# Named places for the temporary tiles of a list-scheduled stretch, with new tables of its plan

## The chip, the cores and the metric

The kernel runs on one core of a Trainium2 chip. The metric is the time of one execution on the device in microseconds. Before the change the median of three runs is 1575.53 us (1574.72 to 1575.8).

## What is computed

Attention in chunks of 64 positions feeds two feed-forward layers of 4608 tokens, width 512 and inner width 2048, the first with h cos h, the second with a sigmoid form of gelu. All of it is in float32.

```python
scores = scale * np.matmul(q_c, k_c.transpose(0, 1, 2, 4, 3))     # 8 batches, 8 heads, 9 chunks of 64
scores = scores - np.max(scores, axis=-1, keepdims=True)
attn = np.exp(scores)
attn = attn / (np.sum(attn, axis=-1, keepdims=True) + 1e-09)
out = np.matmul(attn, v_c)
...
h = x @ w_in
g = h * np.cos(h)
x = g @ w_out
h = x @ moe2_w_in
g = h * (1.0 / (1.0 + np.exp(-1.702 * h)))
out = g @ moe2_w_out
```

## The kernel before

The 4608 tokens are worked on in nine slices of 512. A product in float32 accuracy is made of three: each operand is split in a high and a low part, and high by high, high by low and low by high are summed in PSUM. The kernel begins with a **planned part** (`first_stretch`, up to about 330 us of the trace) and goes on with pairs of slices whose products are formed with fewer multiplications; for these, sums of weight slices ("left factors") and of activations ("right factors") are made ahead.

In the planned part a small list scheduler, the class `Plan`, puts operations on five engines in an order, by an estimated duration of each, a longest path and tables of numbers (`RANK`, `LEAN`, `LEFT` and others). The instructions are then issued in that order, and every engine executes its own in order. The operations are:

- Attention by pairs of token blocks, numbered 0 to 9: scores on TensorE (L395), maximum, subtraction and sum on VectorE (L419, L423, L434), exponentials on ScalarE (L431, or L443 as 16 small ones that give their sums too, for the pairs in `EXP_SUM`), normalisation (L453), transposes on TensorE (L477), their copy by ScalarE (L484, tile `pt`), products with the values (L504, tile `x`). Small products that only keep TensorE working, the fillers (L386), stand ahead of some steps.
- Conversion of 32 weight slices, i0 to i15 of the first layer's w_in and o0 to o15 of its w_out, from float64 bits: absolute value by ScalarE into a temporary tile `wt` (L289), four steps of VectorE (L292, L297, L303, L309), the high part by ScalarE (L320), the low part by VectorE (L326) or, for those in `BY_DMA`, by ScalarE and an adding DMA issued by GpSimd (L331, L334).
- First products `h` (L594, one step of 12 matmuls for each weight slice and token slice) and the cosine (L618 to L633), whose result `r` is stored to memory (`gd<-r`, SyncE, L651).
- Reload ("get", `gt<-gd`, L1565), split in `gh` (ScalarE, L1569) and `gl` (VectorE, L1573), and second products `y` (L686); a flush of the finished `y` goes by VectorE or ScalarE (L713, L715; table `FLUSH`) and a store.
- Left factors: sums of two weight slices (`w32`, L817; `su`, `sw`, L765), split in parts `s_part` (L784, L787) and stored (`wc<-s_part`, L768), with stores of the plain parts beside them (`wc<-i`); later they are loaded back as `w_xh`, `w_xl` (L859). Stores `wo` put the second weights away. Right factors `x_b`, `x_t` and their intermediate `chain` (L887 to L893).
- The plan ends with `joint`: the first products of the first pair of slices (`pb`, `pu`, `pc`, L1191). Their copy by ScalarE (`part<-pb`, L1208) and the sum on VectorE (`part<-pu,part`, L1212) come from code behind the plan, where the order of TensorE is written out and the other engines are ordered by the scheduler of the language.

Temporary tiles of 256 KB (`wt`, `pt`, `r`, `gt`, `yo`, `w32`, `su`, `sw`, `s_part`, `chain`) come from one pool of eight buffers, in the planned part and behind it. The plan counts eight places and does not name them: which buffer a tile gets is settled by the pool, and its first writer waits until the last reader of the tile before it, an engine or a DMA, is done.

## Time and profile before

| what | value |
|---|---|
| median of three runs | 1575.53 us |
| the profiled execution | 1577.51 us |
| its span in the trace | 1575.7 us |
| TensorE busy | 1537.0 us (98%) |
| VectorE busy | 1101.3 us (70%) |
| ScalarE busy | 943.0 us (60%) |
| bytes moved | 414.46 MB, mean 263 GB/s |

The span is the time between the first and the last recorded instruction, the profiled execution's own time is 1.8 us longer. A busy time of 98% says that TensorE sets the length as a whole; it doesn't say in which stretch it waits. For a change to one stretch, the waits of TensorE in that stretch are the view to open, and then what the releaser of the longest wait did itself wait for.

### The profile page before, as it was taken

The page shows a single profiled execution, that of the slowest core. Times are in us where ns is not written, and L with a number is a line of the kernel's source. Part 1 is how long each engine was busy: PE and PEld are TensorE (multiplying, and loading weights), DVE is VectorE, ACT ScalarE, POOL GpSimd, SP SyncE. Part 2 cuts the span into 40 slices and gives each one's busy share as a digit, 9 for nine tenths or more (in the row PEclk, how much of TensorE's full clock was granted, in tenths as well). Part 3 has the DMA queues.
Part 4 walks back from the last instruction along what each step waited for, and adds up shares of the span by engine and source line. Part 5 has one row for each costly group of instructions (what it writes and reads, how often), then busy time and mean ns, then how long its engine had stood idle before and what let it go on. Part 6 is the DMA issues. An engine that isn't in the chain of part 4 may idle for free.

```text
span 1575.7 us, 23982 instructions
## 1 busy us (share of the span) xinstructions
PE 1537.0 (98%) x8919; PEld 1263.8 (80%) x8919; DVE 1101.3 (70%) x1830; ACT 943.0 (60%) x1701; POOL 20.8 (1%) x29
## 2 busy tenths in 40 slices
PE   7799999979999999999999999999999999999998
PEld 6688888768888888788887877888888888888887
DVE  7788876777876787767764886478348834773466
ACT  7788764447775777657773654565356445644453
POOL 0000000000000000000000110000000000000000
PEclk9999999989999999999999999999999999999999
DMA  9753589999888689868989999576667665666663
GB/s 381 261 201 128 160 314 340 335 308 325 307 289 320 228 306 301 334 211 275 321 314 340 315 289 295 214 274 230 218 222 268 210 220 216 239 221 215 231 212 136
DMA packets 141189, 414.46 MB, mean 263 GB/s; under 512 B 13712, under 2 KB 28048, under 8 KB 127760
## 3 DMA queue, kind: packets, MB, share of 16 engines
q1 hardware_dynamic: 137760, 406.90, 73.7%
q0 software_dynamic: 3312, 6.03, 2.1%
q8 instruction: 70, 1.15, 0.3%
q14 instruction: 47, 0.39, 0.1%
HBM read 318.77 MB, written 88.08 MB: 258 GB/s over the span
## 4 chain that ended last, share of the span: by engine, by line
PE 84%; DMA 8%; DVE 5%; ACT 2%; issue 1%; SPq 1%; ACTq 0%; DVEq 0%
PE y L686 20%; PE q L1098 19%; PE pu L1033 11%; PE pu L1191 8%; PE h L594 8%; PE pc L1033 5%; PE pc L1191 4%; PE pb L1033 3%; PE pb L1191 2%; DMA gt<-gd 1%; DMA wc<-s_part 1%; PE x L504 1%; DMA wq<-s_part 1%; PE s L395 1%; DMA raw_o<-w_out 1%
## 5 line engine op out<-in xcount | busy, mean ns | idle before, releaser
L686 PE MATMUL y<-gh,wo 128*128 128x512 f32 x768 | 202.9, 393 | 1.0 <-DMA wo<-wo 1.0
L1098 PE MATMUL q<-gf,w_q 128*128 128x512 f32 x768 | 179.3, 389 | 0.0
L1098 PEld LDWEIGHTS q<-gf,w_q 128*128 128x128 f32 x768 | 144.2, 188 | 29.9
L686 PEld LDWEIGHTS y<-gh,wo 128*128 128x128 f32 x768 | 142.4, 188 | 31.6 <-issue 1.2
L1033 PE MATMUL pu<-x_t,w_s 128*128 128x512 f32 x576 | 141.8, 390 | 0.7 <-DVE part L1008 0.7
L686 PE MATMUL y<-gh,o 128*128 128x512 f32 x512 | 132.6, 393 | 1.2 <-DVE yo L713 1.1
L1015 ACT ACTIVATE g<-part 128x512 f32<-128x512 f32 x96 | 60.5, 631 | 111.1 <-DVE part L1008 111.1
L1033 PEld LDWEIGHTS pu<-x_t,w_s 128*128 128x128 f32 x576 | 108.1, 188 | 23.5 <-DVE part L1008 1.1
L1098 PE MATMUL q<-gh,w_q 128*128 128x512 f32 x384 | 124.2, 389 | 0.0
L686 PEld LDWEIGHTS y<-gh,o 128*128 128x128 f32 x512 | 94.9, 188 | 21.7 <-DVE yo L713 1.6
L686 PE MATMUL y<-gl,wo 128*128 128x512 f32 x384 | 105.9, 390 | 0.0
L1191 PE MATMUL pu<-x_t,w_xh 128*128 128x512 f32 x288 | 90.3, 395 | 7.8 <-DVE part L1212 7.8
L1164 ACT ACTIVATE r<-r 128x512 f32<-128x512 f32 x96 | 60.5, 630 | 41.8 <-DVE r L1161 41.6
L686 PEld LDWEIGHTS y<-gl,wo 128*128 128x128 f32 x384 | 72.1, 188 | 15.7 <-DVE gl L264 0.8
L1098 PEld LDWEIGHTS q<-gh,w_q 128*128 128x128 f32 x384 | 72.1, 188 | 15.0
L594 PE MATMUL h<-xh,i 128*128 128x512 f32 x256 | 83.7, 401 | 0.0
L264 DVE TENSOR_TENSOR gf<-g,gf 128x512 fp32r<-128x512 f32 x68 | 46.9, 692 | 40.4 <-ACT gf L263 40.3
L1098 PE MATMUL q<-gl,w_q 128*128 128x512 f32 x192 | 74.8, 389 | 0.0
L1008 DVE TENSOR_TENSOR part<-pu,part 128x512 f32<-128x512 f32 x64 | 44.2, 691 | 39.6 <-PE pu L1033 21.3
L686 PE MATMUL y<-gl,o 128*128 128x512 f32 x256 | 70.7, 390 | 1.2 <-DVE gl L646 1.2
L1191 PEld LDWEIGHTS pu<-x_t,w_xh 128*128 128x128 f32 x288 | 54.0, 190 | 20.8 <-DVE part L1212 9.6
L1008 DVE TENSOR_TENSOR part<-pc,part 128x512 f32<-128x512 f32 x32 | 22.1, 691 | 63.5 <-PE pc L1033 62.1
(174 smaller groups left out, 3259.0 us busy)
## 6 DMA issues: line engine op xcount, KB each, us to landing
w_s<-wc SPq DMA_DIRECT2D x64, 1024.0 KB, 6.1
w_q<-wq SPq DMA_DIRECT2D x56, 1024.0 KB, 5.0
wo<-wo SPq DMA_DIRECT2D x96, 512.0 KB, 5.2
w_xh<-wc SPq DMA_DIRECT2D x24, 1024.0 KB, 7.1
w_xl<-wc SPq DMA_DIRECT2D x24, 1024.0 KB, 9.3
qk<-qk SPq DMA_DIRECT2D x36, 512.0 KB, 7.1
raw_i<-w_in SPq DMA_DIRECT2D x32, 512.0 KB, 7.6
raw_o<-w_out SPq DMA_DIRECT2D x32, 512.0 KB, 7.7
```

The costliest lines, as they stand in the source:

```text
L264: nc.vector.tensor_tensor(out=lo, in0=src, in1=hi.bitcast(F32), op=ALU.subtract)
L395: nc.tensor.matmul(out=s[e][o0:o0 + CH, w, h, :], lhsT=t[p0:p0 + CH, 0, h, o0:o0 + CH], rhs=t[p0:p0 + CH, 1, h, o0:o0 + CH],)
L504: nc.tensor.matmul(out=xs[i][o0:o0 + CH, b, w, c * CH:(c + 1) * CH], lhsT=t[p0:p0 + CH, c, b, e, :], rhs=pt[p0:p0 + CH, e * (HP // 2) + b, ...
L594: nc.tensor.matmul(out=h, lhsT=a[:, w0], rhs=b[k % 2][:, k // 2] if (layer, j) == (0, 2) else b[:, k, :], start=(k == 0 and i == 0), stop= ...
L686: nc.tensor.matmul(out=ys[d0], lhsT=a, rhs=b, start=(f == 0 and i == 0), stop=(f == NF - 1 and i == 2),)
L1008: nc.vector.tensor_tensor(out=t, in0=more, in1=t, op=ALU.add)
L1015: nc.scalar.activation(out=dest, in_=h, func=AF.Gelu_apprx_sigmoid)
L1033: nc.tensor.matmul(out=o, lhsT=x, rhs=y, start=(m < 3 and k == 0 and n == 0), stop=(m in (1, 5, 6) and k == 1 and n == 2), skip_group_chec ...
L1098: nc.tensor.matmul(out=o, lhsT=x, rhs=y, start=(m < 3 and i == 0 and k == 0), stop=(m in (1, 5, 6) and i == NP - 1 and k == 2), skip_group ...
L1164: nc.scalar.activation(out=r, in_=r, func=AF.Sin, scale=math.pi)
L1191: nc.tensor.matmul(out=out, lhsT=x, rhs=y, start=(start and k == 0 and n == 0), stop=(stop and k == 1 and n == 2), skip_group_check=True,)
```

## The change

Each temporary tile of the planned part now has a named place, `t0` to `t7`. `Plan` chooses it when it puts the operation in the order: of the places that are free, the one that came free first, and a place whose tile is last read by a DMA counts as free when the plan believes the transfer to have landed (before: a fixed 2.0 us after an issue by SyncE, 3.5 by GpSimd). The places form a pool of their own that is closed behind the planned part; a new pool `tmp` of eight buffers is opened behind it on the same memory. The intermediate `chain` of the first pair's t1 moves from a temporary buffer to the pool `ap`. The tables of the plan are new: among them `LEFT` (how far along the second products each left factor begins), `LF_AT` (when the factors are loaded back), `WO`, `FLUSH` (two instead of five flushes by VectorE), `EXP_SUM` (pair 9 is in it now) and `BY_DMA` (eight instead of seven low parts by DMA).

```diff
-    def __init__(self, slots, first=(), lean=None, wait=None):
+    def __init__(self, slots, first=(), lean=None, wait=None, places=(), now=None):
...
+            self.now[:] = [k for k in self.got[o["name"]] if k in self.places]
             for pool in o["drop"]:
-                live[pool if isinstance(pool, str) else self.got[pool[0]][pool[1]]].append(
-                    (t + self.TILE_DMA[eng] if o["size"] else t + cost, done[o["name"]])
-                )
+                k = pool if isinstance(pool, str) else self.got[pool[0]][pool[1]]
+                seen = t + self.TILE_DMA[eng] if o["size"] and k not in self.places else t + cost
+                live[k].append((done[o["name"]] if k in self.places else seen, done[o["name"]]))
...
-        (-9, -7, -5), (-9, -6, -4), (-2, 0.5, 3.5), (6.5, 10, 10),
+        (-9, -7, -5), (-9, -6, -4), (0.5, 1.5, 7), (7, 10.5, 13.5),
...
-    EXP_SUM = (0, 2, 3)
-    BY_DMA = "00010100000000000000011110010000"
-    FLUSH = (0, 0, 1, 0, 1, 1, 1, 1)
-    LEFT = (11, 11, 14, 7, 10, 20, 26, 31)
-    WO, LF_AT = 3, 41
+    EXP_SUM = (0, 2, 3, 9)
+    BY_DMA = "00010100000000010001010101010000"
+    FLUSH = (0, 0, 0, 1, 1, 0, 0, 0)
+    LEFT = (10, 14, 8, 9, 9, 5, 5, 8)
+    WO, LF_AT = 0, 36
...
+    PLACES = [f"t{n}" for n in range(TBUFS)]
+    now, temps = [], {}
+
+    def tmp(shape, dtype, name):
+
+        return temps["pool"].tile(shape, dtype, tag=now.pop(0) if "plan" in temps else "t", name=name)
...
-            c["t"] = tp.tile([P, DM], F32, tag="t", name="wt")
+            c["t"] = tmp([P, DM], F32, name="wt")
...
-                pool, tag = (tp, "t") if layer == 0 else (vp, "v")
-                chain[name, k] = pool.tile([P, N], F32, tag=tag, name="chain")
+                if layer:
+                    chain[name, k] = vp.tile([P, N], F32, tag="v", name="chain")
+                elif ja > J0 or name == "t3":
+                    chain[name, k] = tmp([P, N], F32, name="chain")
+                else:
+                    if k == 0:
+                        chain["both"] = ap.tile([P, 2, N], F32, tag="a", name="chain")
+                    chain[name, k] = chain["both"][:, k]
...
-        slots = dict(t=TBUFS, g=GBUFS, h=2, y0=1, y1=1, y2=1, y3=1, a=2, ap=2, xh=2, xl=2, q=4, v=4)
-        plan = Plan(slots, FIRST, LEAN, WAIT)
+        t = tuple(PLACES)
+        slots = dict(**{k: 1 for k in PLACES}, g=GBUFS, h=2, y0=1, y1=1, y2=1, y3=1, a=2, ap=2, xh=2, xl=2, q=4, v=4)
+        plan = Plan(slots, FIRST, LEAN, WAIT, PLACES, now)
...
-        with tc.manual_schedule():
+        with tc.tile_pool(name="places", bufs=1) as pool, tc.manual_schedule():
+            temps.update(pool=pool, plan=True)
             first_stretch()
+        temps.clear()
+        temps["pool"] = ctx.enter_context(tc.tile_pool(name="tmp", bufs=TBUFS))
```

What the tables move is seen in the order of the engines. In the order's rows a name's number tells tiles of one kind apart, and the changed kernel's lines lie 8 to 15 further down.

ScalarE around the exponentials of pair 3, before (`wt<-raw_i_334` is the conversion of weight i9, the two rows of L443 are the exponentials of pair 3, `pt` the copies of its transposes):

```order
L443 ACT_TABLE_LOAD
L443 ACTIVATE a,ss<-s_812,mx 128x64 x8
L443 ACTIVATE a,ss<-s_813,mx 128x64 x8
L320 ACTIVATE i_915<-wt 128x512
L618 ACTIVATE r<-h 128x512 x2
L320 ACTIVATE i_949<-wt 128x512
L289 ACTIVATE wt<-raw_i_334 128x512
L1569 ACTIVATE gh<-gt 128x512
L627 ACT_TABLE_LOAD
L627 ACTIVATE r<-r 128x512
L630 ACTIVATE r<-r 128x512
L484 ACTIVATE pt<-pt_ps 128x512 x2
```

and in the changed kernel, where that conversion comes first:

```order
L297 ACTIVATE wt<-raw_i_334 128x512
L328 ACTIVATE i_878<-wt 128x512
L451 ACT_TABLE_LOAD
L451 ACTIVATE a,ss<-s_818,mx 128x64 x8
L451 ACTIVATE a,ss<-s_819,mx 128x64 x8
L626 ACTIVATE r<-h 128x512 x2
L328 ACTIVATE i_948<-wt 128x512
L328 ACTIVATE i_951<-wt 128x512
L1584 ACTIVATE gh<-gt 128x512
L635 ACT_TABLE_LOAD
L635 ACTIVATE r<-r 128x512
L492 ACTIVATE pt<-pt_ps 128x512 x2
```

The conversion `wt<-raw_i_334` has moved from behind pair 3's exponentials, and from a place ahead of the copies `pt`, to a place ahead of the exponentials.

SyncE at the end of the planned part, before (`gd2_13` to `gd2_15` are the last gets, `wc0_6` and `wc0_7` the last left factors, `w_xh` and `w_xl` the loads of factors; `wc0_0` is the joint's own factor, `wc0_1` the next):

```order
L1565 DMA gt_3755<-gd2_13_194 128x512
L859 DMA w_xh_3759<-wc0_0_94 128x2048
L859 DMA w_xl_3761<-wc0_0_94 128x2048
L1565 DMA gt_3792<-gd2_14_195 128x512
L768 DMA wc0_6_100<-s_part_3809 128x512
L768 DMA wc0_6_100<-s_part_3810 128x512
L859 DMA w_xl_3889<-wc0_1_95 128x2048
L768 DMA wc0_6_100<-s_part_3824 128x512
L768 DMA wc0_6_100<-s_part_3823 128x512
L1565 DMA gt_3842<-gd2_15_196 128x512
L768 DMA wc0_6_100<-i12_1328 128x512 x2
L768 DMA wc0_6_100<-i13_1518 128x512 x2
```

and in the changed kernel:

```order
L1580 DMA gt_3787<-gd2_13_191 128x512
L776 DMA wc0_6_97<-i12_1515 128x512 x2
L776 DMA wc0_6_97<-i13_1586 128x512 x2
L1580 DMA gt_3823<-gd2_14_192 128x512
L1580 DMA gt_3848<-gd2_15_193 128x512
L776 DMA wc0_7_98<-s_part_3842 128x512
L776 DMA wc0_7_98<-s_part_3843 128x512
L776 DMA wc0_7_98<-s_part_3856 128x512
L776 DMA wc0_7_98<-s_part_3857 128x512
L776 DMA wc0_7_98<-i14_1660 128x512 x2
L776 DMA wc0_7_98<-i15_1745 128x512 x2
```

The loads from `wc0_0` are gone from this stretch (they stand five gets earlier), both last gets stand ahead of the stores of the last left factor, and the loads from `wc0_1` behind them.

ScalarE at the joint, with the semaphores that a row waits on, before:

```order
L1569 ACTIVATE gh_3848<-gt_3792 128x512 [waits DMAHW2_49,PE_49]
L1569 ACTIVATE gh_3863<-gt_3842 128x512 [waits DMAHW0_49,PE_49]
L784 ACTIVATE s_part_3870<-su_3860 128x512 [waits DMAHW7_49,DVE_49,Activation_49]
L784 ACTIVATE s_part_3874<-sw_3861 128x512 [waits DMAHW3_49,DVE_49]
L890 ACTIVATE x_t40_3977<-chain_3675 128x512 [waits DMAHW2_49,DMAHW1_49]
L1208 ACTIVATE part_3903<-pb_3896 128x512 [waits DMAHW4_49,DVE_49,PE_49]
L1208 ACTIVATE part_3928<-pc_3921 128x512 [waits DMAHW6_49,DVE_49,PE_49]
```

and in the changed kernel:

```order
L792 ACTIVATE s_part_3842<-su_3820 128x512 [waits DMAHW2_49,DVE_49]
L792 ACTIVATE s_part_3856<-sw_3821 128x512 [waits DVE_49]
L904 ACTIVATE x_t40_3989<-chain_3649 128x512 [waits DMAHW5_49,DMAHW4_49]
L904 ACTIVATE x_t40_3989<-chain_3649 128x512
L1584 ACTIVATE gh_3868<-gt_3823 128x512 [waits DMAHW0_49,PE_49]
L1584 ACTIVATE gh_3878<-gt_3848 128x512 [waits DMAHW1_49,PE_49]
L1222 ACTIVATE part_3915<-pb_3908 128x512 [waits DMAHW4_49,DMAHW5_49,DMAHW3_49,DMAHW6_49,DMAHW2_49,DMAHW7_49,DVE_49,PE_49]
L1222 ACTIVATE part_3940<-pc_3933 128x512 [waits PE_49]
```

The last parts `s_part` and `x_t` now stand ahead of the last two `gh`, and the copy `part<-pb` waits on six DMA counters instead of one.

## Rows read from the trace of the kernel before

**Rows 1.** Waits of TensorE, 0 to 350 us: engine, line, releaser: total, times, longest

```profile
PE pu L1191 <- DVE part L1212: 7.8, 1, 7.8
...
PE x L504 <- ACT pt L484: 7.3, 4, 5.0
...
PE y L686 <- DVE yo L713: 1.1, 1, 1.1
```

**Rows 2.** Windows: length, busy time of each engine, granted clock, DMA share, GB/s

```profile
60.00:70.00 10.00, 5.26 (x71) 4.37 (x72) 6.49 (x11) 9.06 (x16) 0.00 (x0) 0.70 0.45 133
75.00:205.00 130.00, 130.00 (x856) 106.75 (x847) 109.52 (x189) 104.00 (x179) 4.37 (x5) 1.00 0.50 170
205.00:325.00 120.00, 117.00 (x936) 95.19 (x936) 91.12 (x157) 57.92 (x103) 0.00 (x0) 1.00 0.97 337
345.00:350.00 5.00, 3.79 (x9) 3.02 (x10) 4.38 (x8) 4.97 (x8) 0.00 (x0) 0.50 1.01 364
```

**Rows 3.** Timeline: start, duration, engine, instruction, [idle before <- releaser], 60 to 65 us

```profile
60.41 0.66 ACT L289 ACTIVATE wt<-raw_i 128x512 f32<-128x512 f32 x1 [4.40 <-DMA gd<-r]
...
64.73 2.46 PE L504 MATMUL x<-pt,v 64*64 64x64 f32 x64 [5.01 <-ACT pt L484]
```

**Rows 4.** Chain of waits, 30 to 75 us: start, duration, what

```profile
35.84 5.49 PE h L594 x24
...
41.33 1.16 PE x L504 x64
...
54.25 6.08 DMA gd<-r
...
67.19 7.39 PE h L594 x24
```

**Rows 5.** Timeline around the joint, 331 to 347 us

```profile
331.77 0.61 PE L1191 MATMUL pb<-x_b,w_xh 128*128 128x512 f32 x2
...
334.10 1.48 SPq L1565 DMA_DIRECT2D gt<-gd  x1
...
342.76 0.63 ACT L1569 ACTIVATE gh<-gt 128x512 fp32r<-128x512 f32 x1 [8.07 <-DMA gt<-gd]
...
343.93 2.22 SPq L768 DMA_DIRECT2D wc<-s_part  x4
...
344.85 0.57 ACT L1208 ACTIVATE part<-pb 128x512 f32<-128x512 f32 x1
...
345.46 0.69 DVE L1212 TENSOR_TENSOR part<-pu,part 128x512 f32<-128x512 f32 x1
...
346.21 1.22 PE L1191 MATMUL pu<-x_t,w_xh 128*128 128x512 f32 x2 [7.80 <-DVE part L1212]
```

**Rows 6.** Chain of waits behind the joint, 346 to 352 us

```profile
346.21 2.93 PE pu L1191 x6
349.13 2.17 PE pc L1191 x6
```

**Rows 7.** DMA issues, 200 to 320 us: count, KB each, median us to landing

```profile
gt<-gd SPq DMA_DIRECT2D x35, 256.0 KB, 5.2
...
wc<-s_part SPq DMA_DIRECT2D x24, 256.0 KB, 5.6
```

**Rows 8.** DMA issues, 320 to 350 us

```profile
wc<-s_part SPq DMA_DIRECT2D x8, 256.0 KB, 3.5
gt<-gd SPq DMA_DIRECT2D x3, 256.0 KB, 7.5
```

**Rows 9.** Groups of instructions, 0 to 350 us: count, busy us, mean ns, idle before

```profile
L443 ACT ACTIVATE a<-s,mx 128x64 f32<-128x64 f32 x48 | 14.3, 348 | 4.3 <-DVE mx L437 4.3
...
L297 DVE TENSOR_SCALAR wt<-wt 128x512 uint32<-128x512 uint32 x32 | 13.5, 426 | 0.9
...
L309 DVE SCALAR_TENSOR_TENSOR wt<-raw_i,wt 128x512 uint32<-128x512 uint32 x16 | 11.0, 688 | 0.3
...
L431 ACT ACTIVATE a<-a 128x1024 f32<-128x1024 f32 x7 | 7.5, 1072 | 3.4 <-DVE a L423 3.4
```

More of the change, by code (lines that the diff above doesn't have):

```diff
@@ L779, in hi @@
             if layer == 0:
-                c[k] = [tp.tile([P, DM], F32R, tag="t", name="s_part") for _ in range(2)]
+                c[k] = [tmp([P, DM], F32R, name="s_part") for _ in range(2)]
             else:
@@ L1002, in copied @@
         def copied(src):
[L1003 removed]
+            t = tmp([P, N], F32, name="part")
             nc.scalar.activation(out=t, in_=src, func=AF.Copy)
@@ L1344, in convert_ops @@
             n = (which, f)
-            add((n, 0), "ACT", 0.67, fns[0], [("ld", n), ((which, f - AHEAD[which]), 5)], take="t")
+            add((n, 0), "ACT", 0.67, fns[0], [("ld", n), ((which, f - AHEAD[which]), 5)], take=[t])
             for i, cost in ((1, 0.42), (2, 0.42), (3, KEEP), (4, KEEP)):
@@ L1405, in att_ops @@
                      ("v", p - 1 + w, 1 - w)],
-                    () if first or w else [bank, bank], drop=["t", "v"], rank=RANK[p][2], fill=not first and not w)
+                    () if first or w else [bank, bank], drop=[(("pt", p, w), 0), "v"], rank=RANK[p][2], fill=not first and not w)
             for i in range(2):
@@ L1437, in act_ops @@
             n = ("act", j, f)
-            add((n, 0), "ACT", 0.6, start(0), [("g1", j, f)], take="t")
+            add((n, 0), "ACT", 0.6, start(0), [("g1", j, f)], take=[t])
             add((n, 1), "DVE", KEEP, start(1), [(n, 0)])
```

77 lines of the change are left out of this document (38 added, 39 removed).

## The prediction

> **What bounds the kernel now.** I read the waits of TensorE over the planned part first (0 to 350 us of the trace), since that engine is 98% busy over the whole span and the programs of before and after are the same, instruction for instruction on every engine, once the planned part and the hand-over behind it are past. So the change can move only what TensorE waits for before about 350 us. [rows 1] lists it: one wait of 7.8 us of the joint pair for VectorE, four of together 7.3 us for ScalarE's copies of transposed attention (the longest is 5.0), 1.1 for a flush. From 75 to 205 us TensorE has no idle time at all; from 205 on the transfers are the full resource, 0.97 of the DMA engines' time at 337 GB/s [rows 2].
>
> Then I followed the two long waits back. **The early one** [rows 3, 4]: pair 3's products with the values (L504) start at 64.73 after 5.01 us idle, because ScalarE copied their transposes late, and ScalarE stood before that at 60.41 for a store gd<-r. That store holds a temporary tile. ScalarE executes in order: the conversion wt<-raw_i (the first step of weight i9) had been handed the buffer which the store still read, and gh, the cosines' table load and both copies of pair 3 stood behind it. The chain of waits names it: 6.08 us of gd<-r, then the conversion, and so on to L504. **The late one** [rows 5, 6]: the joint pair's fourth product needs the bank of its second, so the copy of pb (L1208) and the sum L1212. The copy stood on ScalarE behind gh<-gt, which waited 8.07 us for the last get, issued only at 334.10. That get stood on SyncE behind stores of a sum that was not yet made and behind a factor load of 1 MB. gh could begin at 342.76; the joint product had begun at 331.77.
>
> **The change part by part.** (a) *Early.* In the changed order wt<-raw_i_334 (i9) stands ahead of pair 3's exponentials and no longer between them and the copies, and its place is one that a conversion (i3) left long before. The wait of 5.01 us goes. Two costs go with it: the granted clock was 0.70 over 60 to 70 us [rows 2], so that the 64 value products took 2.46 us where the same 64 took 1.16 before [rows 3, 4], 1.3 us, and the 24 products behind them 7.39 where 24 took 5.49 [rows 4], 1.9 us. Together 5.0 + 1.3 + 1.9 = 8.2. Against it: i9's four conversions on VectorE (two of the kind of L297 at 0.43, two of the kind of L309 at 0.69 [rows 9]) now stand ahead of pair 3's normalisation, 2.2 us, and the exponentials start about 1 us later for the conversion ahead of them; part of it is work that VectorE did in the gaps anyway, so pair 3's transposes come, by my estimate, 1.3 us later. Gain 6.9.
>
> (b) *Joint.* In the changed order of SyncE both last gets (gd2_14, gd2_15) stand in front of the last four s_part stores, the factors for the joint are loaded five gets earlier, and the load of the next factor has gone behind. A get is also held by the second products four steps before it, whose last matmul lies 24 matmuls ahead of the joint; at 5.49/24 = 0.229 us each [rows 4] that is 5.5 us ahead. From there a get takes 5.2 us in the median of 200 to 320 us [rows 7] and 7.5 in 320 to 350 [rows 8]: it lands between 0.3 us before and 2 us behind the joint's start. Two gh of 0.63 [rows 5] follow, and ScalarE is free for the copy at the latest 3.3 us behind that start. The copy (0.57) and the sum (0.69) [rows 5] must be done when TensorE has finished 18 joint matmuls and the 6 of y behind them, 24 x 0.229 = 5.5 us, so the copy must start by about 4.1. It holds. Gone are then 7.80 us of idle time and the lower clock behind it: the granted clock was 0.50 from 345 to 350 [rows 2], and twelve matmuls took 2.93 + 2.17 = 5.1 us [rows 6] where 12 x 0.229 = 2.75. Together 7.8 + 2.4 = 10.2.
>
> What stands against (b) is a new wait. The temporary tiles behind the planned part are in a new pool on the same memory, so its first tile, the copy of pb, waits until every place is free: in the changed program the copy waits on six DMA counters where it waited on one, and the latest are the last four s_part stores. They may be issued behind the last get, 5.5 us before the joint at the earliest; with 2.2 us for the four issues [rows 5] and 5.6 [rows 7] or 3.5 us [rows 8] from issue to landing the last of them lands 0.2 to 2.3 us behind the joint's start, and about 5 behind it if their sums come 3 us late. Against 4.1 that is 0 to 1 us; I take 0.5, since the sums' inputs (w32) stand earlier too. Gain 9.7. A rule of the Trainium skill bears on this wait: "DMA: Bandwidth & Descriptors", section "Anatomy of one DMA — SWDGE (gpsimd) path", puts a fixed cost of about 2.0 us on a transfer (there GpSimd's, not SyncE's), most of it the receipt of the write. By that figure a store of 256 KB would land some 2.6 us behind its issue (an estimate from the page) and the wait would be nothing, which would add 0.5 us to the gain; the rows for these very stores are longer, and I stay with them.
>
> (c) *The rest.* The other short waits of before, 1.1 and the 2.3 us left of the 7.3 for L504 [rows 1], may go or not; what replaces them is not in the trace. Three things can bring new ones: pair 9's exponentials go as 16 small ones with their sums, 16 x 0.348 = 5.6 us of ScalarE at most, where one of 1.07 stood [rows 9], and save VectorE two subtractions and a sum; three more flushes on ScalarE stand behind a gh whose get may be late; the two factors (2 MB) ahead of two gets cost up to 3 us of queue if TensorE is just behind. From both sides: 3.4 us gained if all old waits go and none comes, 5 us lost if they stay and two of the three strike. I take a loss of 1.
>
> (d) *The full queue.* An early gain of 7 us asks the transfers of the stretch from 205 us to the joint 7 us sooner, and they were at 0.97. Half of the DMA engines' time was free from 75 to 205 [rows 2], and the changed order has about 2 MB more behind it at the same get (6 us at 337 GB/s) and 1 MB less in all ahead of the last one. So most of the gain passes; I take 1 us off, with bounds of 0 and, if the queue alone sets the pace, 11 (the first rival).
>
> Moves on TensorE itself (first products pulled ahead of attention steps, five fillers fewer, the last pair 22 matmuls earlier) change no count of the products and cost nothing while no wait appears: 0.
>
> Sum: 6.9 + 9.7 - 1 - 1 = 14.6. The profiled execution lasted 1577.5 us, 2.0 more than the median of 1575.5, so 1562.9 for such an execution and **1561** for a median.
>
> **The rivals.** *The queue sets the pace.* From 205 to 325 us the engines of the transfers have nothing left [rows 2], and gets arrive just when they are needed. If so, the last get comes only as much earlier as there is less in front of it, 1 MB or 3 us, and the early gain waits at the joint: gain 3 to 4, a time of 1572. For it speaks the 0.97; against it that half the queue was free before 205 us and that the last get was late through its place on SyncE (issued at 334.10), not through the bytes alone.
>
> *One of the two stays.* A different wait takes the place of the early one (pair 3's copies now stand behind i10's and i11's conversions and a gh whose get is a new tile), or the whole-pool wait at the joint costs as much as the get did. Only the early gain: 1577.5 - 6.9 + 1 = 1571.6, median 1569.5; only the late one: 1577.5 - 9.7 + 1, median 1567.
>
> *Slower: places fixed in advance make ScalarE wait for landings.* Before, a tile took whichever buffer came next; now 92 of 220 temporary tiles take a place whose last reader was a DMA, and the changed plan releases a place only at what it believes to be the landing. Where its belief is short, ScalarE stands in order, as it did at 60.41 [rows 3], and each such stand in the attention stretch costs what that one did, 8.2 us with the clock's share. The stretch of 205 to 325 us is the place, since there a store of a left factor takes 5.6 us to land [rows 7]. Two such stands take back 16.4 of 14.6, so two is the point from which it decides; with three the execution lasts 1577.5 - 14.6 + 24.6 and the median is 1585. Against it: in before too the buffers were taken blind, and from 75 to 325 us TensorE lost 3 us in all [rows 2].
>
> *Not what it says.* The words also say that the plan's end counts more; nothing in the kernel's code but the tables carries that. If the tables suit the real durations worse, gains of (a) and (b) shrink into the cases above; I give it no case of its own.
>
> **How the numbers follow.** Both gains as summed, 1557 to 1566: 0.47. One of the two: 0.25. The queue: 0.11. Slower by stands of ScalarE: 0.11. Better than 1557, with all the small waits of [rows 1] gone too: 0.06. About 0.2%, 3 us, is what a measurement of this kernel can tell from no change; so faster means below 1572.4. That holds for the first, the second and the last case, 0.78, and for some of the queue's: 0.80 faster. The rest of the queue's case, 0.09, is within; 0.11 is slower. The range from 1555 to 1573 takes in the first three cases and leaves out the slower one and a rest on the fast side; the likeliest case alone is 1557 to 1566.
>
> **What would show it.** In the profile after: no idle of ScalarE over 1 us ahead of a wt<-raw_i at 45 to 60 us, and value products of pair 3 at about 59 us and at the full clock, 1.2 us for 64; a first joint product at about 324 us, the copy of pb at most 4.1 us behind it, and no wait above 1 us of pu for VectorE; granted clock 1.00 over the joint. Wrong would be the sum if the copy of pb waits for a wc<-s_part for several us, if the last get still lands 8 us or more behind the joint's start, or if ScalarE shows new waits for gd<-r, wc<-s_part or gt landings with TensorE idle behind them.

## The result and the profile of the changed kernel

The changed kernel's median is 1562.43 us (four runs, 1560.47 to 1564.45), that of the kernel before, run beside it, 1575.66 (1574.72 to 1575.94). The ratio is 0.9917 with a 95% interval from 0.99 to 0.9934, a gain of 13.2 us. The profiled execution lasted 1563.68 us, its span 1561.9. In a second job the same two kernels gave 1562.79 and 1573.66, a ratio of 0.9935 (0.9922 to 0.9947).

The waits of TensorE over 0 to 350 us in the changed kernel (line, releaser: us in total, times, longest) answer to [rows 1]:

```profile
PE pt_ps L485 <- DVE a L461: 3.8, 3, 2.0
PE y L694 <- ACT yo L723: 2.1, 2, 1.6
PE y L694 <- ACT gh L1584: 2.0, 1, 2.0
...
PE x L512 <- ACT pt L492: 0.4, 2, 0.3
```

The wait of `pu` for VectorE (7.8 us) has left the list, and the values' waits for `pt` went from 7.3 to 0.4 us. A new one stands in it: 2.0 us for a `gh`. The windows of the same kernel (length, busy time of PE, PEld, DVE, ACT, POOL, granted clock, DMA share, GB/s) answer to [rows 2]:

```profile
60.00:70.00 10.00, 10.00 (x103) 7.89 (x101) 7.15 (x12) 8.93 (x17) 0.00 (x0) 1.00 0.54 169
75.00:205.00 130.00, 130.00 (x877) 106.89 (x875) 114.02 (x197) 107.95 (x183) 5.47 (x6) 1.00 0.58 193
205.00:325.00 120.00, 115.05 (x854) 92.56 (x855) 91.53 (x162) 61.70 (x136) 0.00 (x0) 0.99 1.00 350
325.00:340.00 15.00, 15.00 (x68) 12.43 (x67) 6.71 (x11) 7.08 (x12) 0.00 (x0) 1.00 0.78 275
```

Three things are to be seen. From 60 to 70 us TensorE is busy throughout and at the full clock, where it had 5.26 us of work and a granted clock of 0.70. Around the joint (325 to 340) it is busy throughout at 1.00, where the clock stood at 0.50 behind the wait. In between, from 205 to 325 us, it got worse: 4.95 us idle instead of 3.0, with the DMA engines at 1.00.

**Lost time.** Stretches of two kernels whose orders differ can't be subtracted by the clock on the wall, so I compare them at equal work: the start of a group of products in the trace, less the time that the matmuls ahead of it in TensorE's order take at the full rate (0.2285 us for each 128 by 512 one, 0.105 for a transpose, 0.0175 for each small one of the scores, 0.11 for a filler). The small products with the values are not taken off; by the same rate of 0.0175 they are 5.6 us at A and 11.2 at B, C and D in every kernel. What is left beyond these is the time that TensorE has lost by then, idle or at a lower clock. Between two kernels at one place the 5.6 or 11.2 drop out, and from B to C and from C to D as well; only a difference from A to a later place holds 5.6 us that were not lost. Place A is the first products behind a pair's values at about 100 us, past the early stretch; B the second products behind the last values, at about 300 us; C the joint's first product; D the third group of joint products, past the wait for the copy of `pb`. The start in the trace stands in brackets. Each figure is of one profiled execution. Executions of one order differ by up to some 2 us here (B is 42.7 and 42.6 in two kernels further down that up to there have the order of the kernel before, whose B is 44.8), so a difference of less than that says little.

| kernel | A | B | C | D |
|---|---|---|---|---|
| before | 33.9 (105.4) | 44.8 (308.4) | 44.9 (331.8) | 56.0 (353.4) |
| changed | 27.3 (98.2) | 38.6 (297.5) | 42.5 (328.8) | 42.4 (339.3) |
| gain up to there | 6.6 | 6.2 | 2.4 | 13.6 |

So 6.6 us were won early and carried for 200 us through a full queue; 3.8 of them were lost between B and C; and 11.2 were won at the joint, which lost 11.1 us before and nothing now. The spans differ by 13.8.

**Early**, in the order of time (start, duration, engine, instruction, idle before in square brackets where there is any), answering to [rows 3]:

```profile
46.85 0.68 ACT L297 ACTIVATE wt<-raw_i 128x512 f32<-128x512 f32 x1
...
59.26 1.07 ACT L492 ACTIVATE pt<-pt_ps 128x512 f32<-128x512 f32 x2
...
63.26 1.16 PE L512 MATMUL x<-pt,v 64*64 64x64 f32 x64
```

The conversion of weight i9 starts at 46.85 without a wait, the copies are done at 60.33, and the 64 value products start at 63.26 without idle time and take 1.16 us instead of 2.46. They could have started 2.9 us earlier: 24 first products now stand between pair 3's transposes and its values, where there were 12.

**At the joint**, answering to [rows 5]:

```profile
317.92 1.67 SPq L1580 DMA_DIRECT2D gt<-gd  x2
321.15 2.64 SPq L776 DMA_DIRECT2D wc<-s_part  x4
...
328.85 0.62 PE L1205 MATMUL pb<-x_b,w_xh 128*128 128x512 f32 x2
...
330.41 0.60 ACT L1222 ACTIVATE part<-pb 128x512 f32<-128x512 f32 x1 [4.35 <-PE pb L1205]
...
331.82 0.69 DVE L1226 TENSOR_TENSOR part<-pu,part 128x512 f32<-128x512 f32 x1 [4.75 <-PE pu L1205]
...
334.29 0.62 PE L1205 MATMUL pu<-x_t,w_xh 128*128 128x512 f32 x2
```

Both last gets are issued 9 to 11 us ahead of the joint and land at 322.38 and 323.02, and the last four `s_part` stores are issued 5.1 to 7.7 us ahead of it. The copy of `pb` waits for TensorE alone and the sum too; the fourth product, which waited 7.80 us, doesn't wait.

**What was lost between B and C** is one wait, on SyncE, ScalarE and TensorE:

```profile
301.05 0.49 SPq L867 DMA_DIRECT2D w_xl<-wc  x1
301.59 0.49 SPq L1580 DMA_DIRECT2D gt<-gd  x1
...
312.27 0.63 ACT L904 ACTIVATE x_t<-chain 128x512 fp32r<-128x512 f32 x1 [2.98 <-DVE chain L901]
312.80 0.61 ACT L1584 ACTIVATE gh<-gt 128x512 fp32r<-128x512 f32 x1
...
313.47 2.80 PE L694 MATMUL y<-gh,o 128*128 128x512 f32 x8 [2.04 <-ACT gh L1584]
```

A get (number 41 of 0 to 47) is issued right behind the two loads of the joint's factors, 2 MB, and lands 10 us later, at 311.6. ScalarE meanwhile stands at an `x_t` ahead of the `gh` in its order, waiting for VectorE's `chain` until 312.27. The windows of 313.4 to 317 and 317 to 321 us, columns as above, give the rest:

```profile
313.40:317.00 3.60, 3.53 (x11) 2.77 (x12) 3.60 (x7) 2.32 (x5) 0.00 (x0) 0.67 1.05 394
317.00:321.00 4.00, 4.00 (x17) 3.25 (x16) 3.12 (x8) 1.66 (x3) 0.00 (x0) 0.87 1.02 379
```

The granted clock is 0.67 and 0.87 behind the idle time, means of stretches that hold both levels, 0.50 (1.2 GHz) and 1.00 (2.4 GHz): 2.04 + 0.33 x 3.6 + 0.13 x 4 = 3.75 us, which is nearly the whole loss of 3.9.

### The profile page after: what moved, and what is told of

Read it like the earlier page. It is cut to its first block, busy times and chain, and to the rows that moved or that the text cites. A ratio compares the mean times of both kernels' runs of the same rounds, so it can differ in the third digit from the quotient of the medians.

```text
span 1561.9 us, 24006 instructions
## 1 busy us (share of the span) xinstructions
PE 1536.9 (98%) x8914; PEld 1263.5 (81%) x8914; DVE 1096.1 (70%) x1824; ACT 948.6 (61%) x1736; POOL 21.9 (1%) x30
## 4 chain that ended last, share of the span: by engine, by line
PE 71%; DVE 4%; DMA 3%; ACT 1%; issue 1%; SPq 0%; DVEq 0%; ACTq 0%
PE q L1112 20%; PE y L694 17%; PE pu L1047 11%; PE pu L1205 8%; PE pc L1047 6%; PE pc L1205 4%; PE pb L1047 3%; PE pb L1205 2%; DMA wo<-wo 1%; DMA o<-wt 1%; DMA x<-y 1%; PE x L512 1%; PE s L403 1%; DMA w<-wc 1%; DVE chain L901 0%
## 5 line engine op out<-in xcount | busy, mean ns | idle before, releaser
L272 DVE TENSOR_TENSOR gl<-g,gh 128x512 fp32r<-128x512 f32 x60 | 41.4, 691 | 33.9 <-ACT gh L271 33.9
```

What stands on the lines that cost most here:

```text
L272: nc.vector.tensor_tensor(out=lo, in0=src, in1=hi.bitcast(F32), op=ALU.subtract)
```

## The experiments

Twelve kernels were run. Each ratio is to runs of the kernel before in the same job. Eight of them take the plan's finished order and move single entries in it before anything is issued, so that the plan itself does not react:

```diff
-            o["fn"]()
+            self.script.append((i, self.fill, list(self.now)))
+        for name, ahead in MOVES:
+            ...
+        for i, self.fill, self.now[:] in self.script:
+            ops[i]["fn"]()
```

Lost time at the four places, in us (D less C is what the joint lost):

| kernel | A | B | C | D | median | ratio (95%) |
|---|---|---|---|---|---|---|
| changed, again | 27.1 | 37.8 | 42.0 | 41.9 | 1562.79 | 0.9935 (0.9922 to 0.9947) |
| after_i9_back | 27.3 | 37.3 | 40.6 | 40.5 | 1563.54 | 0.9939 (0.9925 to 0.9952) |
| after_i9_wait | 28.6 | 39.3 | 41.7 | 41.6 | 1564.41 | 0.9944 (0.9929 to 0.9959) |
| after_rf | 27.9 | 37.5 | 39.4 | 39.3 | 1562.34 | 0.9927 (0.9913 to 0.9941) |
| after_rf_lf | 28.3 | 41.0 | 41.3 | 42.3 | 1561.75 | 0.9918 (0.9905 to 0.9931) |
| after_anon | 28.3 | 41.0 | 49.4 | 49.3 | 1570.27 | 0.9967 (0.9955 to 0.9979) |
| after_old_tables | 29.2 | 37.2 | 39.6 | 52.4 | 1571.94 | 0.9984 (0.9975 to 0.9993) |
| after_left7_late | 27.0 | 41.1 | 45.3 | 50.4 | 1568.41 | 0.9958 (0.9946 to 0.9971) |
| before_i9_early | 31.2 | 41.2 | 41.6 | 52.4 | 1575.43 | 1.0002 (0.9991 to 1.0013) |
| before_v3_late | 28.4 | 37.9 | 38.4 | 48.9 | 1570.48 | 0.9972 (0.9962 to 0.9982) |
| before_get47 | 32.9 | 42.7 | 42.7 | 51.2 | 1573.61 | 0.9991 (0.9981 to 1.0) |
| before_get47_lf | 33.7 | 42.6 | 42.6 | 51.1 | 1574.05 | 0.9993 (0.9984 to 1.0003) |

### The changed kernel again

No edit.

> The changed kernel once more, to see whether its waits repeat and how far its times spread. In its first profile TensorE reaches the joint 2.4 us of waits ahead of the kernel before and lost 3.8 us at 313 us (2.04 us idle behind a gh, and the lower clock behind that). Theory R (the stall at 313 is in the order of the instructions): it is there again, 1.5 to 2.5 us, and the median lies within 1 us of 1562.4. Rival S (it comes and goes with the transfers, and makes the spread from 1560.5 to 1564.5): it is gone or much shorter in this profile.

The wait for `gh` at about 313 us came again (2.4 us instead of 2.0), and the loss from B to C too (4.2). It belongs to the order and not to one execution.

### The early wait: place, position or cover

The prediction gave the early gain to two things at once: i9's conversion stands earlier in ScalarE's order, and its place was freed long before. The first kernel puts the conversion back behind the exponentials, on its named place.

```diff
+MOVES = (
+    ((('i', 9), 0), ('hi', 0)),
+    ((('i', 9), 1), (('act', 0, 3), 4)),
...
```

> The changed kernel, with the conversion of weight i9 moved back to where it stood before the change: on ScalarE behind pair 3's exponentials and ahead of gh and pair 3's copies, its four steps on VectorE behind the normalisation. Its place stays t5, free since i3. Theory P (what cost 8.2 us was the place that a store still read, not the position): within 1 us of the changed kernel, 1561.5 to 1563.5, ScalarE doesn't wait ahead of the conversion. Rival O (the position is what counts): 5 to 7 us slower than the changed kernel, 1567 to 1570.

The conversion, and the value products:

```profile
56.17 0.77 ACT L313 ACTIVATE wt<-raw_i 128x512 f32<-128x512 f32 x1
...
63.28 1.16 PE L528 MATMUL x<-pt,v 64*64 64x64 f32 x64
```

It waits for nothing where it stood in the kernel before. The free place takes the wait away, not the position.

The second kernel does the same and from there on exchanges two places, so that the conversion again takes one that a store still reads:

```diff
+        seen, other = False, dict(t1="t5", t5="t1")
+        for i, self.fill, self.now[:] in self.script:
+            seen = seen or ops[i]["name"] == (('i', 9), 0)
+            if seen:
+                self.now[:] = [other.get(k, k) for k in self.now]
```

> As the run with i9 moved back, but from there on the places t1 and t5 are exchanged, so that i9's tile takes the place which the store of the second cosine result still reads, as it did before the change. That store landed at 58.31 us in the changed kernel's profile. Theory P: ScalarE waits some 2 us for it, and TensorE loses 5 to 8 us as before the change, 1567 to 1570. Rival C (the change also put 24 instead of 12 matmuls between pair 3's transposes and its value products, and that covers the wait): ScalarE waits the 2 us, the copies are done at about 62.6 us, just ahead of the value products at 63.3, and TensorE loses under 1 us: 1562 to 1563.5.

```profile
56.45 1.94 PE L505 MATMUL pt_ps<-ident,a 128*128 128x128 f32 x8 [2.65 <-DVE a L481]
...
59.01 0.67 ACT L317 ACTIVATE wt<-raw_i 128x512 f32<-128x512 f32 x1 [2.97 <-DMA gd<-r]
...
62.05 1.07 ACT L512 ACTIVATE pt<-pt_ps 128x512 f32<-128x512 f32 x2
...
64.55 1.16 PE L532 MATMUL x<-pt,v 64*64 64x64 f32 x64
```

The wait for `gd<-r` is back, 2.97 us of ScalarE, and yet TensorE's value products start without idle time, 1.4 us behind the copies' end; the lost time at A is only 1.3 us higher. The trace puts these 1.3 us elsewhere: at pair 3's transposes TensorE had been idle for 2.65 us (1.14 in after_i9_back), mostly before ScalarE's stand began at 56.04, and the granted clock was 0.53 from 56.4 to 60 us, so that the eight transposes took 1.94 us instead of 1.06. With 24 products as cover, ScalarE's stand costs TensorE no idle time. That gives a third candidate: TensorE's own order. The two kernels that follow do the one and the other in the kernel before. First only the conversion ahead of pair 3's exponentials:

```diff
+MOVES = (
+    ((('i', 9), 0), ('exp', 3, 0)),)
```

> The kernel before, with the first step of weight i9's conversion moved on ScalarE to ahead of pair 3's exponentials, nothing else. Buffers are handed out in turn, so the buffer that the store of a cosine result still reads now falls to the next tile, the second r<-h behind the exponentials, still ahead of pair 3's copies. Theory P (the place that a store reads is what costs): ScalarE waits for the same store one instruction earlier, TensorE is idle 4 to 5 us as before, and the time is within 1 us of the kernel before. Rival O (the position of the conversion): 5 to 7 us faster than before.

```profile
59.79 0.60 ACT L628 ACTIVATE r<-h 128x512 int32<-128x512 f32 x1 [1.92 <-DMA gd<-r]
...
64.57 0.33 PE L514 MATMUL x<-pt,v 64*64 64x64 f32 x2 [1.99 <-ACT pt L494]
```

No gain (1.0002): with buffers handed out in turn, the next tile in the row, an `r`, now meets the store, and the values still wait. Then only TensorE's order: 12 first products ahead of pair 3's values instead of behind them.

```diff
+MOVES = (
+    (('g1', 0, 7), ('v', 3, 0)),)
```

> The kernel before, with the next step of 12 first products put ahead of pair 3's value products on TensorE, so that 24 instead of 12 matmuls lie between its transposes and these; ScalarE still waits for the store. Theory C (the change's order of TensorE covers the wait): the idle time of 5.0 us falls by 2.7 to about 2.3, and part of the lower clock goes; 3 to 5 us faster than before. Rival N (the value products only come later and what waits for them loses as much): within 1 us of before.

```profile
60.08 0.67 ACT L299 ACTIVATE wt<-raw_i 128x512 f32<-128x512 f32 x1 [3.99 <-DMA gd<-r]
...
64.41 0.33 PE L514 MATMUL x<-pt,v 64*64 64x64 f32 x2 [1.89 <-ACT pt L494]
```

ScalarE stands for `gd<-r` as before, 3.99 us, but the time falls by 4.4 us (0.9972), and A by 5.5. Moving twelve matmuls is worth most of the early gain without any named place. What the named places are worth with only twelve products as cover is seen in after_old_tables, below.

### The late wait: the get, the factor loads or the last left factor

The prediction put the joint's wait on SyncE's order: the last get stands behind stores of a sum not yet made and behind a factor load. The first kernel moves that get ahead of them, in the kernel before:

```diff
+MOVES = (
+    (('get', 47), ('lp', 6, 0, 0)),)
```

> The kernel before, with the last get moved on SyncE ahead of the four s_part stores of the last left factor but one and of the 1 MB factor load. Theory G (the place of that get on SyncE is what made the joint wait): it lands at about 335 us instead of 342.7, the copy of pb comes by 338, 7 to 10 us faster than before. Rival W (the next wait is nearly as late): the sum sw still waits for an s_part store that lands at 341.4, the part behind it and the copy of pb come at about 343, 1 to 3 us faster.

```profile
324.94 2.42 SPq L1575 DMA_DIRECT2D gt<-gd  x2
...
337.82 0.63 ACT L794 ACTIVATE s_part<-su 128x512 fp32r<-128x512 f32 x1 [4.22 <-DVE sw L775]
...
339.70 0.60 ACT L1218 ACTIVATE part<-pb 128x512 f32<-128x512 f32 x1 [0.73 <-DVE s_part L797]
...
341.08 1.22 PE L1201 MATMUL pu<-x_t,w_xh 128*128 128x512 f32 x2 [4.59 <-DVE part L1222]
```

The last get, the second of the two in the row, is issued by 327.4 where it was 334.10, its `gh` runs at 332.96, and the copy of `pb` no longer waits for it. It waits for the last left factor instead, whose part `s_part` stands ahead of it on ScalarE and waits 4.22 us for a sum. TensorE still loses 4.59 us there. Of the 11.1 us that the joint loses, 2.6 go; the time falls by 1.4 (0.9991, with an interval that reaches 1.0).

The second is to issue the load of the next factor later (2 MB, of which 1 MB, a `w_xl` at 329.82 in the kernel above, stood among these stores):

```diff
+        load_factors(0, 1)
         return plan
...
-            if i + 1 < NP:
+            if i + 1 < NP and (layer, ja, i) != (0, J0, 0):
```

> As the run before, and the two loads of the next factor (2 MB, of which 1 MB stood ahead of the last get and between the s_part stores) issued behind the plan's own transfers. Theory W: the s_part stores land some 3 us (1 MB) sooner, sw and the copy of pb with them; 4 to 6 us faster than the kernel before, and a wait of pu of 3 to 4 us is left, since the last left factor's sums are begun as late as before. Theory G: no difference to the run with the get moved alone.

What SyncE issued between those stores in its place:

```profile
329.32 0.88 SPq L839 DMA_DIRECT2D wo<-wo  x2
```

0.9993, no difference from the kernel above, and the joint loses the same 8.5. The 4 to 6 us expected from the empty queue did not come, but the queue was not empty either: two stores `wo` of 512 KB each, issued at 344.80 in the kernel above, moved up into the place of the load, so as many bytes stood there as before, and this kernel doesn't test them. The trace of the kernel above gives a bound instead. The store that the sum waited for was issued at 334.31 and landed 3.0 us later, and the quickest of the changed kernel's last four such stores took 2.4 us. By this estimate the bytes ahead of it cost some 0.6 us. The store itself could go no sooner, since its data, a split on VectorE at 333.60, began only behind the landing (333.50) of another `s_part` store, issued at 327.45 ahead of the load.

That left the last left factor itself. In the kernel before its sums begin at 335.32, 3.5 us behind the joint's first product; in the changed kernel, with the new `LEFT`, at 316.65, 12.2 us ahead of it. This kernel puts all its sixteen operations back to just ahead of the joint and leaves the gets where the change has them:

```diff
+MOVES = (
+    (('w32', 7, 0), ('joint',)),
+    (('w32', 7, 1), ('joint',)),
+    (('ls', 7, 0), ('joint',)),
...
+    (('lr', 7, 1), ('joint',)),)
```

> The changed kernel with all operations of the last left factor (sums, parts, stores) moved to the plan's end, behind the last get's gh, where they stood before the change; both last gets stay early. Theory W (the joint's copy waits for the work of that left factor ahead of it on ScalarE and VectorE, and for its stores' landings, since the new pool begins when all places are free): its parts are made at 330 to 331.5 us, its stores land at about 335, the copy of pb comes at 335.5 instead of 330.4, pu waits 2 to 4 us and the lower clock follows: 3 to 6 us slower than the changed kernel. Rival G (the early gets alone are what helped): within 1 us of the changed kernel.

```profile
332.72 2.21 SPq L801 DMA_DIRECT2D wc<-s_part  x4
...
339.18 0.60 ACT L1247 ACTIVATE part<-pb 128x512 f32<-128x512 f32 x1 [5.82 <-DMA wc<-s_part]
...
340.56 0.73 PE L1230 MATMUL pu<-x_t,w_xh 128*128 128x512 f32 x2 [3.28 <-DVE part L1251]
```

The stores are issued 11.6 us later than in the changed kernel, the copy of `pb` waits 5.82 us for their landing, and the joint loses 5.1 us where the changed kernel loses none. The median is 1568.41, by the ratios 3.6 to 6.5 us above the changed kernel's; the figure rises more from A to C too (by 18.3 against 15.2), so not all of it is the joint. I read the wait as that for the whole pool: the first tile behind the plan needs every place free, as the six DMA counters on this copy say. The wait is real, and the change hides it by making the last left factor early. No kernel was run with the last left factor late and the pool kept open, nor one with the early left factor alone in the kernel before, so neither has a price by itself.

### The two halves: naming and tables

The changed order without the names: one pool of eight buffers handed out in turn, as before, in the planned part and behind it.

```diff
-        return temps["pool"].tile(shape, dtype, tag=now.pop(0) if "plan" in temps else "t", name=name)
+        return temps["pool"].tile(shape, dtype, tag="t", name=name)
...
-        with tc.tile_pool(name="places", bufs=1) as pool, tc.manual_schedule():
-            temps.update(pool=pool, plan=True)
+        temps["pool"] = ctx.enter_context(tc.tile_pool(name="tmp", bufs=TBUFS))
+        with tc.manual_schedule():
             first_stretch()
-        temps.clear()
-        temps["pool"] = ctx.enter_context(tc.tile_pool(name="tmp", bufs=TBUFS))
```

> The changed kernel with its order, but with the temporary tiles of the planned part taken from one pool of eight buffers in turn, as before the change; the same pool goes on behind the plan. Theory T (the order that the new tables give carries the gain, the names of the places little): 1561 to 1565, as the changed kernel; ScalarE stands at a second r<-h at about 58 us for the store of a cosine result, and the 24 matmuls between pair 3's transposes and value products cover it. Rival N (the named places carry it): waits of tiles for stores come back in the early part and near the joint, 6 us slower or more, 1569 and up.

0.9967, 1570.27 us. The early gain stays (A 28.3) and so does the joint's, but 8.4 us are lost from B to C. The chain of waits there (start, duration, what):

```profile
296.80 8.62 DMA wc<-s_part
...
305.51 0.71 DVE s_part L795
...
306.66 0.38 SPq L1580
...
308.60 10.32 DMA gt<-gd
```

A split `s_part` on VectorE has been handed the buffer that a store still reads, 8.62 us from issue to landing. Its own store stands in order on SyncE, and behind it a get, issued at 306.66 where the changed kernel issues it at 299.57. This get and the next one land 6.2 and 7.3 us later than in the changed kernel, where TensorE itself is 2.4 us behind at B, and TensorE waits. (The pool that isn't closed also lets two loads of the next weights, `raw_i`, in among these gets, at 298.29 and 318.93; what part of the 8.4 is theirs was not separated.)

The names with the tables of before:

```diff
-    EXP_SUM = (0, 2, 3, 9)
...
-    LEFT = (10, 14, 8, 9, 9, 5, 5, 8)
-    WO, LF_AT = 0, 36
+    EXP_SUM = (0, 2, 3)
...
+    LEFT = (11, 11, 14, 7, 10, 20, 26, 31)
+    WO, LF_AT = 3, 41
...
```

> The changed kernel's code with all tables of the kernel before: named places, the new rule for when a place comes free and t1's chain in its new pool, but none of the new numbers. Theory T: the joint waits as before, since the last left factors and gets are ordered by the old numbers (the last left factor's sums begin only behind the last second products), and one of the early waits at most goes: 1569 to 1577. Rival N (the named places carry the gain): 1560 to 1566.

```profile
PE pu L1205 <- DVE part L1226: 5.8, 1, 5.8
...
PE pb L1205 <- DMA w_xh<-wc: 2.3, 1, 2.3
PE pb L1205 <- DMA w_xl<-wc: 1.6, 1, 1.6
...
341.03 0.60 ACT L1222 ACTIVATE part<-pb 128x512 f32<-128x512 f32 x1 [3.54 <-DMA wc<-s_part]
```

(Three rows of TensorE's waits and one of the timeline.) 0.9984, 1571.94 us. Early, the places alone do it, with i9's conversion and the 12 products of cover where the kernel before had them:

```profile
56.01 0.69 ACT L297 ACTIVATE wt<-raw_i 128x512 f32<-128x512 f32 x1 [0.38 <-DVE i L334]
...
59.07 1.07 ACT L492 ACTIVATE pt<-pt_ps 128x512 f32<-128x512 f32 x2
...
59.71 0.33 PE L512 MATMUL x<-pt,v 64*64 64x64 f32 x2 [0.35 <-ACT pt L492]
```

The conversion doesn't wait for a store, and the values begin at 59.71 after 0.35 us idle. A is 29.2, 4.7 less than before, and the gain stays to B (37.2). But the joint loses 12.8: the copy of `pb` waits for the stores of a late left factor, as in after_left7_late, and the factor `w_xl` comes 1.6 us late; `w_xh` was 2.3 us late already, which is the loss from B to C. So the names, with the new rule for when a place is free and the chain in its new pool, give 2.5 us and the tables without names 5, by these ratios; together they gave 10 and 13 in the two jobs. Each covers a loss that the other's gain runs into: the tables need names for the full stretch ahead of the joint, and the names need the early left factor for the wait at the joint.

### The wait at 313 us

Two attempts on the loss from B to C. The first issues the `x_t` of the fourth right factor behind the plan, so that ScalarE no longer stands there ahead of the `gh`:

```diff
+        for k in range(2):
+            right_factor(0, J0, 3, k)
...
-  ...for f in RIGHT_B[6:]
+  ...for f in RIGHT_B[8:]
```

> The changed kernel, with the right factor x_t of the joint's fourth product (written behind the plan, and put by the scheduler among the plan's last instructions) issued directly behind the plan's own operations, in order. In the changed kernel's profile ScalarE stood at 312.27 us 2.98 us for VectorE's chain with this x_t, gh behind it came late and TensorE lost 3.8 us. Theory R: that wait goes, 3 to 4 us faster than the changed kernel, 1558.5 to 1559.5. Rival Q (the transfers are the limit there, the gets come no earlier): gh waits for its get instead and the time is within 1 us of the changed kernel. Rival L (x_t is then late for the joint): pu waits for x_t behind the joint's 24 matmuls, 1 to 3 us, and the gain is eaten.

```profile
310.92 0.63 ACT L1586 ACTIVATE gh<-gt 128x512 fp32r<-128x512 f32 x1 [2.09 <-DMA gt<-gd]
...
311.60 2.14 PE L694 MATMUL y<-gh,o 128*128 128x512 f32 x8 [1.30 <-ACT gh L1586]
```

The wait falls from 2.04 to 1.30 us, the loss from B to C from 3.9 to 1.9, and now the `gh` waits for the get itself. The order on ScalarE was half of it, the 2 MB ahead of the get the other half. The second kernel also moves the factor loads behind two more gets:

```diff
+MOVES = (
+    (('lf',), ('lp', 6, 0, 0)),)
```

> The run with x_t issued behind the plan, and the load of the joint's two factors (2 MB) moved on SyncE from ahead of get 41 to behind get 43. In the run with x_t moved alone gets 41 and 42 landed 0.7 and 1.1 us later than TensorE could have used them, 10 us behind their issue, and TensorE lost 1.3 us and some clock at 313 us. Theory L (the 2 MB ahead of those gets): both land 4 to 6 us sooner, no wait is left at 313 us, TensorE reaches the joint 2 to 3 us earlier than with x_t moved alone, and 4 to 6 earlier than in the changed kernel; 1557 to 1560. Rival J (the factors now land too late for the joint): pb waits for w_xl 1 to 3 us, nothing is gained.

The get now lands at 308.2, some 5 us ahead of its use, there is no wait, and the loss from B to C is 0.3. The place is understood. The medians don't show it, though: 1562.34 and 1561.75, ratios 0.9927 and 0.9918, whose intervals overlap the changed kernel's. The second execution lost 3 us elsewhere (B is 41.0, through waits of transposes for VectorE at about 273 us, whose length differs from execution to execution) and 1.0 at the joint, where `pu` waits for ScalarE's `part`. Neither is shown to be faster than the changed kernel.

## Why the prediction held, and where its reasons did not

The prediction was 1561 us, in a range of 1555 to 1573; 1562.43 came. Its sum for such an execution was 1562.9, and the profiled one took 1563.68. That the total came so near is in part luck: the joint gave 1.5 us more than its term, and the rest and the queue took 2.2 us more than theirs. By its steps:

- **(a) Early, 6.9 predicted, 6.6 measured.** The size held, and its terms with it: the idle time is gone, the value products take 1.16 us, the transposes come 0.9 us later (55.90 to 56.78) where the estimate was 1.3. At equal work TensorE has lost 1.4 us more than before at these transposes and loses 8.0 less from there to A, where the prediction had 1.3 and 8.2. The reason was half right. after_i9_back shows that the place counts and not the position in the order. That place alone is enough: after_old_tables, with the position and the twelve products of before, lies 4.7 us lower at A. But it is not needed either. The moves on TensorE, which the prediction priced at 0, cover most of the wait by themselves: before_v3_late has only twelve matmuls moved and lies 5.5 lower at A, and after_i9_wait has ScalarE's wait back without idle time of TensorE behind it. The two causes overlap almost wholly; both together give 6.6. The prediction looked at how long ScalarE was late and not at how much work TensorE had in hand meanwhile. It also said value products at about 59 us; they stand at 63.26, since 24 products are ahead of them.
- **(b) Joint, 9.7 predicted, 11.2 measured.** The size held; the cause named was only the first of two. It was the step "that get stood on SyncE behind stores of a sum that was not yet made" that failed as an explanation: before_get47 takes exactly that away, and of the 11.1 us at the joint 2.6 go (1.4 in the time). Behind the get the last left factor was nearly as late, and it was the next to arrive. Nor were the gets held as the prediction had it, by the second products four steps before: the last one was issued at 319.27, while the products of that step ran until about 323.4, and it landed 5.8 us ahead of the joint, where the prediction had 0.3 us ahead at best. That rule orders the plan; the program doesn't wait for it. What the change does about the left factor is to make it earlier, and after_left7_late shows what that is worth in the changed kernel, 5 us of the joint. The whole-pool wait, taken at 0.5 us within 0 to 1, cost 0 in the changed kernel, 5.82 of ScalarE's time and 3.28 of TensorE's where the stores come late, and with the old tables 3.54 of ScalarE's, ahead of a wait of TensorE of 5.8. It was rightly named as what stands against the gain. The 1.5 us more are that 0.5 and a loss of 1.0 within the joint's first twelve products, of which 0.7 is a wait for `w_xl` that the sum left out; with the factors loaded five gets earlier it is gone. In the waits of the kernel before, 328 to 352 us:

```profile
PE pb L1191 <- DMA w_xl<-wc: 0.7, 1, 0.7
```

- **(c) and (d) The rest and the full queue, -2 predicted, -4.2 measured.** The mis-sized term. One of the three things named in (c), "the two factors (2 MB) ahead of two gets cost up to 3 us of queue", is the one that struck, at 313 us, together with an `x_t` on ScalarE that was not named: 3.8 us from B to C where the whole of (c) was taken at 1. It is also why the first joint product came at 328.85 and not at about 324: of the 6.6 us won early, 2.4 were left there. after_rf and after_rf_lf take it away in two halves. The queue itself, (d), took 0.4 us of the early gain between A and B, though the DMA share went from 0.97 to 1.00.
- **The rivals.** That the queue sets the pace did not happen: the gain of 6.6 us at A was 6.2 at B, 200 us later. One of the two stays: neither did, but before_get47 and after_left7_late show how near it was, since without the early left factor the joint keeps 5 to 8.5 us of its loss. Slower by waits for landings: the mechanism exists, but on the other side of the change. It is in after_anon, with buffers handed out in turn, that a tile has to wait for a store of 8.6 us and the stretch loses 8.4 us. In the changed kernel the longest such wait of the stretch from 205 us takes 1.01 us (VectorE's `su` at 274.39, for `wc<-s_part`), and I found none of TensorE's longer waits there that leads back to one. Earlier there is one that the prediction would have priced at up to 8.2 us:

```profile
84.28 0.60 ACT L626 ACTIVATE r<-h 128x512 int32<-128x512 f32 x1 [2.50 <-DMA gd<-r]
```

  ScalarE stands 2.50 us for a store of a cosine result there, with named places, and TensorE has no idle time from 75 to 205 us. Such a stand costs what TensorE lacks in cover, here nothing.

The rule of the Trainium skill that was weighed in (b), a fixed cost of about 2.0 us on a transfer ("DMA: Bandwidth & Descriptors", section "Anatomy of one DMA — SWDGE (gpsimd) path"), gave an estimate of 2.6 us for a store of 256 KB. The changed kernel's DMA issues (count, KB each, median us to landing) at 320 to 332 us, and at 200 to 320, say:

```profile
wc<-s_part SPq DMA_DIRECT2D x4, 256.0 KB, 2.7
...
wc<-s_part SPq DMA_DIRECT2D x28, 256.0 KB, 5.2
```

The last four stores come near the page's figure, and the same store in the full stretch takes twice that. That the fixed cost is the reason for the 2.7 us is not shown: each of the four had three transfers of 256 KB still to land ahead of it, and the landings follow each other 0.6 to 0.9 us apart. The prediction stayed with the rows of the full stretch, and the page's figure was nearer here.

What stays open: what the whole-pool wait and the early left factor are worth each by itself; whether the 2.7 us by which before_i9_early lies lower at A than before, with the same time at the end, are more than the spread of executions, and whether a kernel without the wait at 313 us measures faster than the changed one.

## What to carry to other kernels

When an engine that executes in order waits long, list what arrives second and third there before you price the removal: taking the latest away was worth 2.6 us at a place that lost 11.1. Look at both ends of a wait, the late producer and the work the consumer has in hand: twelve matmuls put ahead of the values gave about as much there as the free buffer did (5.5 and 4.7 us). And where buffers are handed out in turn, a plan that reckons durations but not which buffer a tile gets can meet a store's landing anywhere; naming the places keeps the order's gain (5 to 8 us here), but the first tile behind a closed pool waited here for the last store, so the last store must be made early.

## What the runs showed that had not been expected

- The time from issue to landing of the same 256 KB store went from 2.7 us (320 to 332 us of the changed kernel) over 5.2 in the median of 200 to 320 us to 8.62 in after_anon's chain, and a get of the same size took 10.32 us there. A fixed allowance in a plan, such as the 2.0 us of the old one, is short by two to four times in the full stretch.
- The price of the lower clock behind a wait can be nearly as large as the wait: 2.04 us of idle time at 313 us cost 3.75, since the granted clock was 0.67 and 0.87 in the two stretches behind it.
- An early gain of 6.6 us passed through 120 us in which the DMA engines were at 1.00, and lost 0.4.
- Executions of one kernel spread more than the first runs showed (the kernel before 1574.72 to 1575.94 over 4 runs, and 1570.92 to 1577.36 over 30 in a later job), so differences of 2 us between experiments needed the lost time at single places to be read at all.
